# Attention, mixture of experts and gated MLP on one core: the sums of the weights' blocks as GpSimd additions and subtractions instead of adding DMAs and negated copies

## The chip, the cores and the metric

One core of a Trainium2 chip runs the whole program. The metric is device time in microseconds (us), the median of several executions. The engines are named as the profile names them: PE (TensorE; PEld is its weight load), DVE (VectorE), ACT (ScalarE), POOL (GpSimd) and SP (SyncE, which only starts DMAs here).

## The reference, cut to what matters

```python
def reference(q, k, v, moe_w_gate, moe_w1, moe_w2, moe2_w_gate, moe2_w_val, moe2_w_out):
    attn = block_causal_attention(q, k, v)          # 4 batches, 8 heads, 576 positions, head size 64
    x = attn.transpose(0, 2, 1, 3).reshape(2304, 512)
    # mixture of experts: 8 experts, 512 -> 1024 -> 512
    P = np.exp(x @ moe_w_gate - max)                # 8 rounds of normalising rows, then columns
    out = np.zeros((2304, 512), dtype=np.float32)
    for e in range(8):
        h = np.maximum(x @ w1[e], 0.0)
        ye = h @ w2[e]
        out += P[:, e:e + 1] * ye
    # gated MLP: 512 -> 1536 -> 512, weights in float64
    g = out @ w_gate
    return (g / (1 + np.exp(-g)) * (out @ w_val)) @ w_out
```

## The kernel before

The large products are done by a scheme of Strassen and Winograd: a 2x2 arrangement of blocks is multiplied with seven products of blocks instead of eight. For that, four blocks of the weights (`W11`, `W12`, `W21`, `W22`, each 128 partitions x 512 float32) have to be combined into sums `T1` to `T4`. Every operand is then split into a high and a low float16 part: ACT writes the high part (line 146), DVE the low part (line 147), and PE multiplies high by high, high by low and low by high.

The program has three stages. In the first (0 to about 450 us of the span) attention runs, with products of the first two weight units filled in. In the second (about 450 to 1730 us), called the expert stage here, a loop over 14 weight units (half an expert each) interleaves two streams on PE: `products_in` (line 507, into the PSUM tiles `abc`) and `products_out` (line 615, into the tiles `m_o`). A third stream, `Background`, prepares the next unit's weights and, a share per unit, the weights of the gated MLP: one of its small tasks is issued at a step of the loop. The third stage (1730 us on) is the gated MLP.

The order of instructions on each engine is fixed when the program is written out; each engine takes its own in that order and waits on semaphores. A task list per set of weights does this: the loads (`wr`, four DMAs from SP, line 338); four reductions on DVE to the largest value (`wmx`, line 342); `across_begin` (line 101, DVE writes a diagonal, `w_d`, `gg_d`, `gv_d` or `go_d`) and `across_mid` (line 108, a PE product that spreads the maximum over the partitions), so that PE waits in its queue for DVE there; then the scale, and then `sum_tasks` (line 250), which makes the sums in place, each as an adding DMA that POOL issues, between the splits:

```python
        def add(o, x):
            nc.gpsimd.dma_start(o, x, accum_op=ALU.add)
```

An adding DMA can only add, so two of the four blocks are negated by ACT beforehand (`minus`, line 314). A set has five sums. There are 30 sets of expert weights (tiles `wr`) and 9 of the gated MLP (tiles `f_g`, `f_v`, `f_o`; there the operands go back to DRAM by DMAs that SP issues, line 445, `scr_g<-gg`).

POOL also issues the adding DMAs that add each expert's result to the output sum `acc` (lines 1399 and 1411, `acc<-ev_s` and `acc<-ev`). Temporary tiles come from one pool, `Places`, in order of release: who takes a place waits until its last user is done, and that is often one of these DMAs.

Of the kernel before, what the change touches and what calls it, by code (L numbers as in the profile page):

```python
# [13 lines left out]
AF = mybir.ActivationFunctionType  # L14
ALU = mybir.AluOpType
# [10 lines left out]
W11, W21, W22, T4, T1, T2, T3 = range(7)  # L26
# [4 lines left out]
def attention_moe_glu_kernel(  # L31
# [21 lines left out]
    nc = tc.nc  # L53
# [44 lines left out]
    def across_begin(mx, n, name):  # L98
        d = (small if n == 1 else pairs[0]).tile([P, n, P], F32, tag=f"dg{n}", name=f"{name}_d", bufs=1)
        for i in range(n):  # L100
            nc.vector.tensor_scalar_mul(d[:, i], ident, mx[:, i : i + 1])
        return {"d": d, "n": n, "name": name}
# [15 lines left out]
    def pow2_end(g, n, top, name, root=False):  # L118
        r2 = small.tile([P, n], F32, tag=f"sm{n}", name=f"{name}_m")
        nc.vector.tensor_scalar_max(r2, across_end(g), 1e-30)  # L120
        e = small.tile([P, n], F32, tag=f"se{n}", name=f"{name}_e")
        if root:
            nc.vector.tensor_scalar(
                e.bitcast(I32), r2.bitcast(I32), 1, EXPONENT, op0=ALU.logical_shift_right, op1=ALU.bitwise_and
            )
        else:
            nc.vector.tensor_single_scalar(e.bitcast(I32), r2.bitcast(I32), EXPONENT, op=ALU.bitwise_and)
        inv = small.tile([P, n], F32, tag=f"si{n}", name=f"{name}_i")
        nc.vector.tensor_scalar_mul(inv, e, 2.0 ** (-top + (64 if root else 0)))
        s = small.tile([P, n], F32, tag=f"ss{n}", name=f"{name}_s")  # L130
        nc.vector.reciprocal(s, inv)
        return s, inv
# [117 lines left out]
    def sum_tasks(b, sp, name, flip):  # L250

        los = {}

        def add(o, x):
            nc.gpsimd.dma_start(o, x, accum_op=ALU.add)  # L258

        def up(o, src, minus=False):  # L260
            los[o] = sp(o, src, minus)

        def low(o, *gone):
            los.pop(o)()
            places.give(*gone)

        def t0():
            up(W11, b[0][0])

        def t1():  # L270
            low(W11)
            add(b[0][0], b[0][1])
            up(W21, b[1][0], True)

        def t2():
            low(W21)
            add(b[1][0], b[1][1])
            up(W22, b[1][1])

        def t3():  # L280
            low(W22)
            add(b[0][1], b[1][1])

        def t5():
            up(T1, b[0][0], True)
            add(b[1][0], b[0][0])

        def t6():
            low(T1)
            add(b[1][1], b[0][0])  # L290

        def t8():
            up(T3, b[0][1])

        def t9():
            low(T3, b[0][1])
            up(T4, b[1][0], True)
            places.give(b[0][0])

        def t10():  # L300
            low(T4, b[1][0])
            up(T2, b[1][1], flip)

        gap = (0, None, 0)
        return (
            [(1, t0, 0), (1, t1), (1, t2), (0, t3)]
            + [gap] * 1
            + [(1, t5, 0), (0, t6)]
            + [gap] * 2
            + [(1, t8, 0), (1, t9), (1, t10), (0, lambda: low(T2, b[1][1]))]  # L310
        )

    def minus(x):
        nc.scalar.activation(x, x, AF.Copy, scale=-1.0)

    units, made = {}, set()

    def expert_items(u):


        e, f0 = divmod(u * FU, FF)
        inv = small.tile([P, 2], F32, tag="winv", name=f"winv_{u}")
        iw = small.tile([P, 1], F32, tag="iw", name=f"iw_{u}")
        W1, W2 = {}, {}
        units[u] = (W1, W2, iw)
        items = []
        for i, W in enumerate((W1, W2)):
            g = {"b": [[None, None], [None, None]]}

            def load(g=g, i=i):  # L330
                for r in range(2):
                    for c in range(2):
                        b = g["b"][r][c] = places.take(f"wr_{u}_{i}_{r}{c}", F32, main=False)
                        if i == 0:
                            src = w1[e][r * TB : (r + 1) * TB, f0 + c * TB : f0 + (c + 1) * TB]
                        else:
                            src = w2[e, f0 + r * TB : f0 + (r + 1) * TB, c * TB : (c + 1) * TB]
                        nc.sync.dma_start(b, src.rearrange("(k p) f -> p k f", p=P))
                g["mx"] = small.tile([P, 4], F32, tag="wmx", name=f"wmx_{u}_{i}")

            def mx(k, g=g, sums=i == 0 or u >= 2):
                nc.vector.tensor_reduce(
                    g["mx"][:, k : k + 1], g["b"][k // 2][k % 2], axis=AX.XY, op=ALU.max, apply_absolute_value=True
                )
                if sums and k > 1:
                    minus(g["b"][(k - 1) // 2][(k - 1) % 2])

            def begin(g=g, i=i):
                m1 = small.tile([P, 1], F32, tag="wm1", name=f"wm1_{u}_{i}")
                nc.vector.tensor_reduce(m1, g["mx"], axis=AX.X, op=ALU.max)  # L350
                g["r"] = across_begin(m1, 1, f"w{u}{i}")

            def end(g=g, i=i):
                s, iv = pow2_end(g["r"], 1, -1 if i == 0 else 0, f"w{u}{i}")
                g["s"] = small.tile([P, 2], F32, tag="ws", name=f"ws_{u}_{i}")
                nc.vector.tensor_copy(g["s"][:, 0:1], s)
                nc.vector.tensor_scalar_mul(g["s"][:, 1:2], s, -1.0)
                nc.vector.tensor_copy(inv[:, i : i + 1], iv)
                if i == 1:
                    nc.vector.tensor_mul(iw, inv[:, 0:1], inv[:, 1:2])  # L360

            def sp(o, src, minus=False, g=g, i=i, W=W):
                W[o] = places.take(f"w{i}_{u}_{o}", main=False)
                return split_later(W[o][:, 0], W[o][:, 1], src, g["s"][:, minus : minus + 1])

            tasks = [(0, lambda k=k, mx=mx: mx(k), 1) for k in range(3)]
            tasks += [(0, lambda mx=mx, begin=begin: (mx(3), begin()), 1)]
            tasks += [(0, lambda g=g: across_mid(g["r"]), 1), (0, end, 1)]
            if i == 1 and u < 2:

                def plain_sp(r, c, g=g, sp=sp):
                    sp((r, c), g["b"][r][c])()
                    places.give(g["b"][r][c])

                tasks += [(1, lambda r=r, c=c, f=plain_sp: f(r, c)) for r in range(2) for c in range(2)]
            else:
                tasks += sum_tasks(g["b"], sp, f"w{i}_{u}", i == 1)
            tasks.append((0, lambda i=i: made.add((u, i))))
            items.append((4, load, tasks))
        return items  # L380
# [3 lines left out]
    def glu_items(name, src, rawp):  # L384
# [5 lines left out]
        g = {}  # L390
# [11 lines left out]
        def mx(b, r, c):  # L402
            k = 2 * r + c
            if k == 0:
                g["mx"] = small.tile([P, 4], F32, tag="wmx", name=f"gmx_{name}")
            nc.vector.tensor_reduce(
                g["mx"][:, k : k + 1], b[r][c], axis=AX.XY, op=ALU.max, apply_absolute_value=True
            )
# [41 lines left out]
        for t, r, c in quads:  # L450
            if (r, c) == (0, 0):
                b = [[None, None], [None, None]]
            cur = {}

            def last(cur=cur, b=b, r=r, c=c):
                mx(b, r, c)

            def first(cur=cur, b=b, q=(t, r, c)):
                exponent(cur, b, *q)
                if q[1:] == (1, 0):  # L460
                    minus(b[0][1])
                elif q[1:] == (1, 1):
                    minus(b[1][0])

            tasks = [(1, first, 0)]
            tasks += [(0, lambda cur=cur: (shift(cur), sign(cur))), (0, lambda cur=cur: mantissa(cur)), (0, last, 2)]
            if (r, c) == (1, 1):
                tasks[-1] = (0, lambda last=last, t=t: (last(), begin(t)))
                tasks += [(0, lambda: across_mid(g["r"]), 0), (0, lambda t=t: end(t))]
                tasks += sum_tasks(b, lambda o, src, minus=False, t=t: sp(t, o, src, minus), f"g{name}_{t}", name == "o")  # L470
            items.append((0, lambda cur=cur, q=(t, r, c): load(cur, *q), tasks))
# [1250 lines left out]
```

## Time and profile before

| what | value |
|---|---|
| median of 3 executions | 2221.84 us (2218.31 to 2226.15) |
| the profiled execution's own time | 2215.86 us |
| its span | 2214.0 us |
| PE busy | 1991.7 us (90%) |
| DVE busy | 1556.1 us (70%) |
| ACT busy | 1409.3 us (64%) |
| POOL busy | 783.4 us (35%) |
| mean granted clock of PE | 0.969 of full speed |

The time is that of the slowest (here the only) core; the span is the profiled part of it. An engine's busy time is the sum of its instructions, so 90% for PE says that about 222 us of the span pass without a matmul; it does not say what PE waits for then. The granted clock is PE's speed as a share of 2.4 GHz; it has two levels, 1.0 and 0.5 (2.4 and 1.2 GHz).

### The profile page before, as it was taken

What the parts mean: (1) busy time and instruction counts of PE and PEld (TensorE: products, weight loads), DVE (VectorE), ACT (ScalarE), POOL (GpSimd) and SP (SyncE); (2) the same over time, 40 slices, a digit from 0 to 9 for tenths busy, and PEclk for the clock granted to TensorE, in tenths of its full rate; (3) what the DMA queues carried; (4) which work ended last, traced back from release to release, by engine and by line L of the source; (5) the groups of instructions that cost most, each with busy time, mean ns of one, the idle gap of its engine ahead of it and who ended that gap; (6) DMA issues with size and microseconds to landing.
All of it is one profiled execution on the core that took longest, in us unless ns stands there. A gap on an engine that the chain in (4) does not pass through costs nothing. (4 is left out here: it accounts for less than half of the span.)

```text
span 2214.0 us, 47787 instructions
## 1 busy us (share of the span) xinstructions
PE 1991.7 (90%) x18378; PEld 1692.8 (76%) x18378; DVE 1556.1 (70%) x3466; ACT 1409.3 (64%) x3018; POOL 783.4 (35%) x1068
## 2 busy tenths in 40 slices
PE   6789899898989889898998988889898998999997
PEld 3457667787778778787887877778787887888887
DVE  6886774776667666677676677677666787656766
ACT  5666665476767767677776776777677556544442
POOL 4634443123434444444443453434344123100100
PEclk8899999999999999999999999999999999999999
DMA  6533322537898988999898998979889310110212
GB/s 169 129 95 101 105 82 76 136 70 146 167 183 176 182 158 160 188 174 201 148 167 180 173 193 173 190 144 172 181 165 200 94 44 1 44 58 16 63 39 48
DMA packets 196803, 287.56 MB, mean 130 GB/s; under 512 B 19552, under 2 KB 88800, under 8 KB 196576
## 3 DMA queue, kind: packets, MB, share of 16 engines
q0 software_dynamic: 94640, 158.51, 43.2%
q1 hardware_dynamic: 101936, 126.01, 18.8%
q8 instruction: 144, 2.36, 0.4%
q14 instruction: 83, 0.68, 0.1%
HBM read 90.98 MB, written 24.38 MB: 52 GB/s over the span
## 5 line engine op out<-in xcount | busy, mean ns | idle before, releaser
L507 PEld LDWEIGHTS <-w 128*128 128x128 f16 x6720 | 619.7, 100 | 120.2 <-issue 51.9
L615 PEld LDWEIGHTS <-m_h 128*128 128x128 f16 x5292 | 521.2, 99 | 90.4 <-issue 23.0
L507 PE MATMUL abc_m_b<-xs,w 128*128 128x256 f16 (+1 forms) x3840 | 486.8, 268 | 22.4 <-ACT m_t L532 10.0
L1411 POOL DMA_DIRECT2D acc<-ev x351 | 339.6, 1056 | 322.3 <-ACT ev L1418 203.3
L615 PE MATMUL m_o_b<-w,m_h 128*128 128x256 f16 x3024 | 409.7, 275 | 19.3 <-ACT ev L1418 14.6
L615 PE MATMUL m_o_ac<-w,m_h 128*128 128x256 f16 x2268 | 317.3, 277 | 1.1 <-ACT ev L1418 1.1
L147 DVE SCALAR_TENSOR_TENSOR w<-wr,ws,w 128x512 f16<-128x512 f32 x210 | 158.0, 755 | 129.1 <-ACT w L146 124.5
L507 PE MATMUL abc_m_c<-xs,w 128*128 128x256 f16 (+1 forms) x1920 | 230.2, 263 | 16.6 <-ACT m_r L743 13.5
L258 POOL DMA_DIRECT2D wr<-wr x150 | 141.0, 942 | 226.0 <-DMA wr<-wr 72.9
L1418 ACT ACTIVATE ev<-m_o_b,pe 128x256 f32<-128x256 f32 x351 | 161.7, 476 | 74.0 <-PE m_o_b L615 55.8
L146 ACT ACTIVATE w<-wr,ws 128x512 f16<-128x512 f32 x210 | 151.1, 721 | 47.9 <-DMA wr<-wr 34.9
L1418 ACT ACTIVATE ev<-m_o_ac,pe 128x256 f32<-128x256 f32 (+1 forms) x234 | 135.2, 581 | 47.6 <-DMA acc<-ev 23.9
L156 DVE TENSOR_TENSOR m_h<-m_t,m_h 128x512 f16<-128x512 f32 (+1 forms) x210 | 132.8, 635 | 39.6 <-ACT m_h L653 39.0
L650 DVE SCALAR_TENSOR_TENSOR m_h<-m_t,m_h 128x512 f16<-128x512 f32 (+1 forms) x210 | 131.6, 634 | 13.2 <-ACT m_h L646 12.8
L1399 POOL DMA_DIRECT2D acc<-ev_s x65 | 81.1, 1248 | 164.9 <-ACT ev_s L1395 144.1
L966 POOL TENSOR_SCALAR e<-e,r 128x64 f32<-128x64 f32 (+2 forms) x144 | 80.3, 582 | 159.5 <-DVE r L961 100.2
L646 ACT ACTIVATE m_h<-m_t 128x512 f16<-128x512 f32 (+1 forms) x210 | 121.2, 582 | 24.4 <-DVE m_t L529 7.7
L653 ACT CAST m_h<-m_t 128x512 f16<-128x512 f32 (+1 forms) x210 | 122.2, 582 | 20.0 <-DVE m_t L674 9.2
L507 PEld LDWEIGHTS <-gg_w 128*128 128x128 f16 x1260 | 114.0, 98 | 22.7 <-issue 10.7
L615 PEld LDWEIGHTS <-g_h 128*128 128x128 f16 x1134 | 110.5, 98 | 18.4 <-issue 5.4
L507 PEld LDWEIGHTS <-gv_w 128*128 128x128 f16 x1260 | 113.6, 98 | 12.7 <-issue 1.2
L507 PE MATMUL abc_m_a<-xs,w 128*128 128x256 f16 (+1 forms) x960 | 122.0, 269 | 0.0
(320 smaller groups left out, 3463.1 us busy)
## 6 DMA issues: line engine op xcount, KB each, us to landing
acc<-ev POOLq DMA_DIRECT2D x351, 256.0 KB, 5.4
wr<-wr POOLq DMA_DIRECT2D x150, 256.0 KB, 4.5
wr<-in_w_dram SPq DMA_DIRECT2D x128, 256.0 KB, 5.6
acc<-ev_s POOLq DMA_DIRECT2D x52, 256.0 KB, 5.2
st<-hl SPq DMA_DIRECT2D x48, 144.0 KB, 3.5
raw_g<-in_w_gate_dram SPq DMA_DIRECT2D x12, 512.0 KB, 6.0
raw_v<-in_w_val_dram SPq DMA_DIRECT2D x12, 512.0 KB, 5.7
raw_o<-in_w_out_dram SPq DMA_DIRECT2D x12, 512.0 KB, 5.5
```

Source lines behind the costliest of these rows:

```text
L146: nc.scalar.activation(hi, src, AF.Copy, scale=s)
L147: return lambda: nc.vector.scalar_tensor_tensor(lo, src, s, hi, op0=ALU.mult, op1=ALU.subtract)
L156: nc.vector.tensor_sub(lo, src, hi)
L258: nc.gpsimd.dma_start(o, x, accum_op=ALU.add)
L507: nc.tensor.matmul(ps[:, f], W[o][:, sh, k, f * P : (f + 1) * P], xs[:, o, mh, k, c0 : c0 + n], start=x not in begun, stop=True, skip_grou ...
L615: nc.tensor.matmul(ps, h[o][:, sh, k, ii * P : (ii + 1) * P], W[o][:, mh, k], start=o in (X11, X12) and k == 0 and j == 0, stop=True, skip ...
L646: nc.scalar.activation(hi, src, AF.Relu)
L650: nc.vector.scalar_tensor_tensor(lo, src, 0.0, hi, op0=ALU.max, op1=ALU.subtract)
L653: nc.scalar.copy(hi, src)
L1399: nc.gpsimd.dma_start(acc[:, x - ii : x + 1, cols], e[:, :n], accum_op=ALU.add)
L1411: nc.gpsimd.dma_start(acc[:, x], e, accum_op=ALU.add)
L1418: nc.scalar.activation(e[:, cols], ps, AF.Copy, scale=p)
```

## The change

The five sums of a set are made by `tensor_tensor` on POOL, in place, in the same order and at the same places of the task list. Since this operation can subtract, the negated copies on ACT go, and the sign of one split (`W21`) changes with them.

```diff
-        def add(o, x):
-            nc.gpsimd.dma_start(o, x, accum_op=ALU.add)
+        def total(o, x, y, op):
+            nc.gpsimd.tensor_tensor(o, x, y, op=op)
...
         def t1():
             low(W11)
-            add(b[0][0], b[0][1])
-            up(W21, b[1][0], True)
+            total(b[0][0], b[0][0], b[0][1], ALU.subtract)
+            up(W21, b[1][0])
 
         def t2():
             low(W21)
-            add(b[1][0], b[1][1])
+            total(b[1][0], b[1][1], b[1][0], ALU.subtract)
             up(W22, b[1][1])
 
         def t3():
             low(W22)
-            add(b[0][1], b[1][1])
+            total(b[0][1], b[1][1], b[0][1], ALU.subtract)
 
         def t5():
             up(T1, b[0][0], True)
-            add(b[1][0], b[0][0])
+            total(b[1][0], b[1][0], b[0][0], ALU.add)
 
         def t6():
             low(T1)
-            add(b[1][1], b[0][0])
+            total(b[1][1], b[1][1], b[0][0], ALU.add)
...
-    def minus(x):
-        nc.scalar.activation(x, x, AF.Copy, scale=-1.0)
...
-                if sums and k > 1:
-                    minus(g["b"][(k - 1) // 2][(k - 1) % 2])
...
-                if q[1:] == (1, 0):
-                    minus(b[0][1])
-                elif q[1:] == (1, 1):
-                    minus(b[1][0])
```

On POOL, the five sums of the third set of the gated MLP's first weight stood as DMAs between the additions to `acc` (`f_g_00` is the block in row 0, column 0). Before:

```order
L258 DMA f_g_00_10492<-f_g_01_10969 128x512
L1411 DMA acc<-ev_1_2_0_12189 128x512
L258 DMA f_g_10_11048<-f_g_11_12109 128x512
L1411 DMA acc<-ev_1_3_0_12198 128x512
L258 DMA f_g_01_10969<-f_g_11_12109 128x512
L258 DMA f_g_10_11048<-f_g_00_10492 128x512
L258 DMA f_g_11_12109<-f_g_00_10492 128x512
L1399 DMA acc<-ev_1_s_12335 128x2x256
```

The same place of the changed kernel:

```order
L258 TENSOR_TENSOR f_g_00_10468<-f_g_00_10468,f_g_01_10943 128x512
L1402 DMA acc<-ev_1_2_0_12157 128x512
L258 TENSOR_TENSOR f_g_10_11022<-f_g_11_12078,f_g_10_11022 128x512
L1402 DMA acc<-ev_1_3_0_12166 128x512
L258 TENSOR_TENSOR f_g_01_10943<-f_g_11_12078,f_g_01_10943 128x512
L258 TENSOR_TENSOR f_g_10_11022<-f_g_10_11022,f_g_00_10468 128x512
L258 TENSOR_TENSOR f_g_11_12078<-f_g_11_12078,f_g_00_10468 128x512
L1390 DMA acc<-ev_1_s_12303 128x2x256
```

No instruction has moved; each of the 195 sums stands where its DMA stood, and its operand is now computed by POOL itself. On ACT, the place in the expert stage where the third block of the first set of the gated MLP is taken up (line 425), before:

```order
L1418 ACTIVATE ev_1_12_4_7048<-m_o_1_1_ac,pe_6640 128x256
L425 ACTIVATE f_g_10_7059<-raw_g_10_6979 128x512
L314 ACTIVATE f_g_01_6981<-f_g_01_6981 128x512
L1395 ACTIVATE ev_1_s_7074<-m_o_1_0_b,pe_6640 128x256
L646 ACTIVATE m_2_h_7085<-m_2_t_7039 128x512
```

And now, where later lines have numbers that are smaller by 5 or 9:

```order
L1409 ACTIVATE ev_1_12_4_7038<-m_o_1_1_ac,pe_6630 128x256
L420 ACTIVATE f_g_10_7049<-raw_g_10_6969 128x512
L1386 ACTIVATE ev_1_s_7063<-m_o_1_0_b,pe_6630 128x256
L637 ACTIVATE m_2_h_7074<-m_2_t_7029 128x512
```

One copy of 128x512 has gone; there are 78 of them in the program. The rows of PE, DVE and SP are the same in both kernels.

## Rows read from the trace of the kernel before

**Rows 1.** Windows, the expert stage: busy us and instructions of each engine.

```profile
core 0: us, PE busy (x) PEld busy (x) DVE busy (x) ACT busy (x) POOL busy (x), PEclk, DMA share, GB/s
450.00:1730.00 1280.00, 1151.53 (x10643) 1014.47 (x10642) 893.58 (x1759) 910.87 (x1851) 534.12 (x591) 0.97 0.88 171
```

**Rows 2.** PE's waits in the expert stage: us in total, times, longest.

```profile
PE m_w L108 <- DVE w_d L101: 44.4, 13, 6.3
PE m_o_b L615 <- ACT ev L1418: 14.6, 17, 3.8
PE abc_m_c L507 <- ACT m_r L743: 13.5, 7, 2.9
PE abc_m_b L507 <- ACT m_t L532: 10.0, 11, 2.8
PE m_gg L108 <- DVE gg_d L101: 9.1, 3, 3.5
PE m_go L108 <- DVE go_d L101: 8.8, 3, 3.3
PE abc_m_b L507 <- DVE m_t L529: 7.3, 6, 1.9
PE m_gv L108 <- DVE gv_d L101: 7.0, 3, 3.0
```

**Rows 3.** Timeline, 882 to 915 us: start, us, engine, line, [idle before <-releaser].

```profile
882.30 17.52 SPq L445 DMA_DIRECT2D scr_g<-gg  x7
890.07 0.86 POOL L258 DMA_DIRECT2D f_g<-f_g  x1 [2.98 <-DMA f_g<-f_g]
894.14 0.86 POOL L258 DMA_DIRECT2D f_g<-f_g  x1 [3.22 <-PE m_o_b L615]
900.00 7.22 SPq L338 DMA_DIRECT2D wr<-in_w_dram  x4
915.03 0.80 PE L108 MATMUL m_w<-w_d,ones 128*128 128x128 f32 x2 [5.17 <-DVE w_d L101]
```

**Rows 4.** Windows of PE around that wait: us, PE busy, granted clock, DMA share, GB/s.

```profile
905.00:916.00 11.00, 5.83 (x49) 0.90 1.08 243
916.00:921.00 5.00, 5.00 (x36) 0.53 0.28 48
```

**Rows 5.** The page's DMA queues and issues: the software queue, and one sum's DMA.

```profile
q0 software_dynamic: 94640, 158.51, 43.2%
wr<-wr POOLq DMA_DIRECT2D x150, 256.0 KB, 4.5
```

**Rows 6.** Windows of lines 258 (POOL) and 314 (ACT) in the expert stage.

```profile
450.00:1730.00 1280.00, 160.90 (x175) 0.97 0.88 171
450.00:1730.00 1280.00, 43.27 (x70) 0.97 0.88 171
```

**Rows 7.** Waits of POOL and ACT in the expert stage.

```profile
POOL wr L258 <- DMA wr<-wr: 68.6, 38, 6.1
ACT w L146 <- DMA wr<-wr: 33.9, 28, 4.2
```

**Rows 8.** The chain that ended last in the expert stage, shares of 1280 us by line.

```profile
by line: issue 4.0%; DMA wr<-wr 3.9%; DMA acc<-ev 3.5%; DMA acc<-ev_s 2.2%; DMA f_o<-f_o 1.8%; PE abc_m_b L507 1.5%; PE m_o_b L615 1.3%; POOL acc L1411 1.3%; PE m_o_ac L615 1.0%; DMA wr<-in_w_dram 0.6%; ACT ev L1418 0.6%; DMA raw_o<-in_w_ou
```

**Rows 9.** POOL's groups by line and shape: busy us, mean ns | idle before.

```profile
L1589 POOL TENSOR_TENSOR g_t<-v_t,g_t 128x512 f32<-128x512 f32 x12 | 15.3, 1272 | 1.3 <-DVE v_t L529 1.2
```

**Rows 10.** DVE's groups with two SBUF inputs: the largest and the seventh.

```profile
L147 DVE SCALAR_TENSOR_TENSOR w<-wr,ws,w 128x512 f16<-128x512 f32 x210 | 158.0, 755 | 129.1 <-ACT w L146 124.5 <-PE m_o_b L615 2.6 <-PE m_o_ac L615 1.6
...
L156 DVE TENSOR_TENSOR m_h<-m_r,m_h 128x512 f16<-128x512 f32 x56 | 38.3, 684 | 2.0 <-ACT m_h L653 2.0
```

**Rows 11.** Timeline at 1824 us: an operation on POOL and one on DVE.

```profile
1824.42 1.27 POOL L1589 TENSOR_TENSOR g_t<-v_t,g_t 128x512 f32<-128x512 f32 x1 [1.22 <-DVE v_t L529]
1824.98 1.27 DVE L1591 TENSOR_TENSOR g_t<-v_t,g_t 128x512 f32<-128x512 f32 x1
```

**Rows 12.** Line 1591 on DVE, all: ns shortest/median/longest.

```profile
L1591 DVE TENSOR_TENSOR g_t<-v_t,g_t x30: 424/692/1266, 1820.6 to 2193.4; 128x512 f32<-128x512 f32 x24, 128x256 f32<-128x256 f32 x6
```

More of the change, by code (lines that the diff above doesn't have):

```diff
@@ L339, in load, with mx @@
                 g["mx"] = small.tile([P, 4], F32, tag="wmx", name=f"wmx_{u}_{i}")
-            def mx(k, g=g, sums=i == 0 or u >= 2):
+            def mx(k, g=g):
                 nc.vector.tensor_reduce(
```

## The prediction

> **What bounds the kernel now.** I read the busy shares by window first. In the expert stage PE is busy for 1151.5 of 1280 us at a mean granted clock of 0.97, while DVE (894), ACT (911) and POOL (534) are far from full; the DMA engines, on the other hand, are busy for 0.88 of the time [rows 1]. So PE is the bound with holes in it: 1280 - 1151.5 = 128.5 us without a matmul, and a clock of 0.97 costs another 0.03 x 1280 = 38 us. These 167 us are all that this change can win in the stage; the reader should see that the sums lie almost entirely in it (175 of 195) [rows 6].
>
> Next, what PE waits for. The largest part is `across_mid`, whose product waits for DVE to have found the maximum of newly loaded weights: 44.4 + 9.1 + 8.8 + 7.0 = 69.3 us. The next is ACT being late to empty PSUM: 14.6 + 13.5 + 10.0 = 38.1 us in the three largest rows; DVE being late to do so costs 7.3 us [rows 2]. Then I followed one of the long waits back. The product at 915.03 waited 5.17 us for DVE, and DVE for weights whose loads SP had begun to issue at 900.00 and finished 7.2 us later; ahead of them in SP's queue stood seven stores of `gg`, from 882.30 to 899.8; and the last of these stores hang on the last sums, of which POOL issued the fourth after 2.98 us of waiting for an earlier sum's DMA and the fifth after another 3.22 us [rows 3]. (That row names PE as releaser; the product that it names runs all the time, so I take it for the DMA.) Behind the fifth sum in POOL's queue stands an addition to `acc` (the rows of the change show it), whose end frees a place. Between 905 and 916 us the DMA engines are full (1.08), and after the wait the clock is at its lower level, 1.2 GHz, for most of 5 us (0.53) [rows 4]: a long wait is paid for twice.
>
> Last, the chain of waits. From about 1376 us, where it can be followed, to 1730, flights of sums make 3.9% + 1.8% = 5.7% of 1280 us, 73 us, and flights of additions to `acc` 3.5% + 2.2% = 5.7%, as much [rows 8]. The expert stage is thus a PE-bound pipeline that hiccups on DMA latency, and the sums are about half of the latency in that chain.
>
> **What goes.** 175 DMAs of 256 KB in the stage. A sum takes 4.5 us from issue to landing [rows 5]. The software queue took 43.2% of the engines' span for 158.5 MB, and 195 sums move 51.1 MB, which is 32% of it: 0.139 x 2214 = 308 us of all engines, 277 us of it in the stage. The DMA share there should fall from 0.88 to about 0.66. POOL's waits for sums, 68.6 us for `wr` alone, go, and with them the delay of the additions to `acc` behind them; ACT's wait of 33.9 us for them goes as well [rows 7]. ACT also loses 70 copies, 43.3 us [rows 6]; ACT is not the bound, so this counts only through its lateness.
>
> **What comes.** 195 POOL operations of 128x512 float32. The nearest row has the same shape and two SBUF inputs: 1.27 us [rows 9]. The 175 in the stage take 222 us against 161 us for issuing the DMAs [rows 6], so POOL rises from 534 to about 595 of 1280 us. Hidden by POOL's idle time; behind one addition stands at most 1.27 - 0.92 = 0.35 us more, against some 4.5 us less for whoever waits for the sum. The releasers of each sum stay the same splits; no new wait for another engine arises.
>
> The price that the rows do show is DVE's. At 1824.42 us POOL begins a two-input operation; DVE's own two-input operation, begun at 1824.98, takes 1.27 us and ends 0.56 us after POOL's does [rows 11], where its median is 0.69 us [rows 12]. So DVE stands still until POOL is done if both its inputs are in SBUF.
>
> How much is that? Seven groups with two SBUF inputs, from line 147 (158.0 us) to line 156 (38.3 us), 158.0 + 114.9 + 114.5 + 76.7 + 38.7 + 38.5 + 38.3, take 579.6 us, almost all in the stage [rows 10]. At some 0.7 us each these are about 830 in 1280 us, so 0.8 begin within 1.27 us, and each waits half of it on average: about 0.5 us per sum, 88 us of DVE time. Bounds: none (sums that fall into DVE's gaps) and 222 us (all of each). DVE has 386 us idle in the stage, so it does not become the bound; what counts is how much reaches PE. Its lateness to empty PSUM costs PE only 7.3 us today [rows 2], against 894 us of work. I take 12 us, about a seventh; bounds 0 and 88.
>
> In the row it is DVE that waits; POOL's twelve operations of that shape have a mean of 1272 ns, one price for all [rows 9]. The Trainium skill ("SBUF — State Buffer", section "Who interferes with whom") goes further and speaks against this change: between a VectorE instruction with two SBUF inputs and a GpSimd one that reads SBUF, the one that starts second is blocked fully, whichever it is. By that rule a sum that meets DVE at such an operation (579.6 of 1280 us, 0.45 of the time) would first wait for its end and then hold up the next one for its whole 1.27 us: 0.45 x 1.27 + 0.55 x 0.5 = 0.85 us per sum, 148 us of DVE in place of 88, and at the same seventh 21 us of PE, so 9 us more than the sum below.
>
> **The sum,** against the profiled execution's own 2215.9 us. Of the 69 us at `across_mid` I take 40% back, 28 us: the sums are about half of the DMA latency in the chain, but loads and `acc` additions stay. Of the 38 us of clock a third, 12 us, since the slow stretches follow such waits. Of ACT's lateness (38.1 us in the three rows, about 50 with the smaller ones) 30%, 15 us, for the freed copies and waits. Less 12 us for DVE. Bounds of the three gains together: nothing, if loads and `acc` additions alone set the waits, and 69 + 38 + 50 = 157 us if all such waits went. Sum: -28 - 12 - 15 + 12 = -43 us, 2173 us. The 20 sums before 450 us I cost at nothing: POOL's idle time there hides 0.35 us each; without that cover it is 7 us. The profiled execution was 6 us under the median of the runs, so the forecast on their scale is about **2179 us**.
>
> **The rivals.**
> - *It is worth more.* If the sums' flights are what makes the additions to `acc` late too (they stand behind them in POOL's queue and share the DMA engines at 0.88), most of the waits go: 70% of 157 us less 12 gives -98 us, 2124. For it: the waits of POOL [rows 7]; against: the additions to `acc` keep two thirds of the software queue's bytes [rows 5], and the loads stay.
> - *No difference.* The loads wait for places which `acc` additions free, and these wait for ACT, which waits for PE; then shorter sums only make gaps elsewhere. The gains are 12 us, and DVE's price takes them: 2222. For it: half of the chain's flights are not sums [rows 8].
> - *Slower.* DVE's blocking reaches PE. Place: the two-input operations of lines 147, 650, 156 and 674, behind which the operations that empty PSUM (529, 544) stand in DVE's queue. Price: if half of the upper bound, 111 us, arrives at PE against 55 us of gains, +56, 2278; if the 88 us of my estimate arrive, +33, 2255. It decides from 55 / 175 = 0.31 us of PE per sum. Against: in the last stage line 1591's median of 692 ns says that few of its operations are hit [rows 12].
>
> **How the numbers follow.** A measurement of this kernel tells about 0.3% (7 us) from no change. Forecast (-20 to -70 us) 0.45; worth more 0.15; no difference (-20 to +15) 0.20, of which 0.08 lies beyond 0.3% on the fast side and 0.02 on the slow side; slower 0.20. So faster 0.68, same 0.10, slower 0.22. The range leaves out about half of the "worth more" case below 2128 and half of the slower one above 2242. The forecast's own range is 2150 to 2200.
>
> **What would show it.** Right: the stage's DMA share near 0.66; no POOL wait for sums; `across_mid`'s waits near 40 us; a clock of 0.98; DVE busy up by some 90 us in the stage, with maxima near 1.9 us at line 147; POOL's sums at 1.27 us. Wrong: POOL's sums far above 1.27 us because DVE blocks them in turn; `across_mid`'s waits unchanged, which would make the loads' places the cause; or PE's waits for DVE at lines 529 and 544 grown to tens of us.

## The result and the profile after

The changed kernel takes 2246.11 us (median of 4 executions, 2242.41 to 2251.30) against 2223.99 us of the kernel before (4 executions, 2218.31 to 2228.66): a ratio of 1.0102, 95% interval 1.007 to 1.0135. It is slower by 22 us, where 2179 us was forecast and the range ended at 2242. The profiled execution has a span of 2245.0 us, an own time of 2246.76 us and a mean granted clock of 0.960.

The page's busy times come first; they answer to the small table of before.

```profile
PE 2005.3 (89%) x18378; PEld 1697.6 (76%) x18378; DVE 1742.3 (78%) x3466; ACT 1377.8 (61%) x2940; POOL 882.5 (39%) x1068
```

PE's time without a matmul rose from 2214.0 - 1991.7 = 222 us to 2245.0 - 2005.3 = 240 us, and its busy time by 14 us at the same number of matmuls, which goes with the lower mean clock (0.969 before, 0.960 now). What stands out is DVE: the same operations as before take 1742.3 - 1556.1 = 186 us more, 0.95 us for each of the 195 sums. The window of the expert stage answers to [rows 1] (it ends 10 us later here).

```profile
450.00:1740.00 1290.00, 1151.27 (x10601) 1009.56 (x10599) 1061.45 (x1755) 871.44 (x1758) 615.67 (x582) 0.96 0.65 131
```

The DMA share fell from 0.88 to 0.65, as forecast, and PE's clock did not rise: 0.96 against 0.97. Next the page's row for the software queue, which answers to [rows 5], and that of an addition to `acc`, which stood at 5.4 us before.

```profile
q0 software_dynamic: 66560, 107.37, 29.2%
...
acc<-ev POOLq DMA_DIRECT2D x351, 256.0 KB, 4.3
```

So the DMA side did what it should. PE's waits in the expert stage, which answer to [rows 2], show where the time went instead.

```profile
PE m_o_b L606 <- ACT ev L1409: 38.3, 14, 5.9
PE m_w L108 <- DVE w_d L101: 35.2, 18, 4.3
PE abc_m_b L498 <- DVE m_t L520: 32.6, 21, 5.6
PE m_go L108 <- DVE go_d L101: 7.8, 3, 3.3
PE m_gv L108 <- DVE gv_d L101: 7.4, 3, 2.9
PE m_gg L108 <- DVE gg_d L101: 6.8, 3, 3.7
PE abc_m_c L498 <- ACT m_r L734: 3.9, 5, 0.9
PE abc_m_b L498 <- ACT m_t L523: 3.3, 2, 1.8
```

Lines have moved by 9: 498, 520, 606 and 1409 are the former 507, 529, 615 and 1418. `across_mid` fell from 69.3 to 35.2 + 7.8 + 7.4 + 6.8 = 57.2 us. The wait for ACT's emptying of `m_o` went from 14.6 to 38.3 us, that for DVE's of `abc` from 7.3 to 32.6 us, and both have single waits of over 5 us, which they had not before.

What makes DVE late is seen in its groups (busy us, mean ns | idle before) and in all instructions of two lines (shortest/median/longest ns); the first group answers to [rows 10].

```profile
L147 DVE SCALAR_TENSOR_TENSOR w<-wr,ws,w 128x512 f16<-128x512 f32 x210 | 201.8, 966 | 75.0 <-ACT w L146 73.6
L641 DVE SCALAR_TENSOR_TENSOR m_h<-m_t,m_h 128x512 f16<-128x512 f32 x168 | 150.4, 903 | 1.1 <-ACT m_h L637 0.9
...
L665 DVE SCALAR_TENSOR_TENSOR m_t<-m_t,m_t 128x512 f32<-128x512 f32 x112 | 100.5, 897 | 0.8
L339 DVE TENSOR_REDUCE wmx<-wr 128x1 f32<-128x512 f32 x128 | 84.7, 678 | 11.3 <-DMA wr<-in_w_dram 11.1
...
L520 DVE TENSOR_TENSOR m_t<-m_t,abc_m_b 128x512 f32<-128x512 f32 x64 | 43.6, 681 | 26.2 <-PE abc_m_b L498 22.0 <-ACT ev L1409 3.2
```

```profile
L147 DVE SCALAR_TENSOR_TENSOR w<-wr,ws,w x210: 734/747/5931, 27.6 to 1745.3; 128x512 f16<-128x512 f32 x105
L665 DVE SCALAR_TENSOR_TENSOR m_t<-m_t,m_t x140: 410/683/4448, 479.1 to 1826.5; 128x512 f32<-128x512 f32 x112, 128x256 f32<-128x256 f32 x28
L258 POOL TENSOR_TENSOR wr<-wr,wr x150: 1253/1584/2921, 28.9 to 1736.4; 128x512 f32<-128x512 f32 x150
```

Operations with two SBUF inputs grew (line 147 from a mean of 755 to 966 ns, line 641, formerly 650, from 688 to 903). Those with one SBUF input (line 339) or one from PSUM (line 520) kept theirs, 678 and 681 ns. The median of line 147 is still 747 ns, and its longest takes 5.93 us: the price does not come as a little for each operation. Counted in DVE's timeline, 35 operations take 2 us or more, 133.6 us together, where none did before. They hold about half of what DVE lost; the rest lies in about 110 shorter stops. POOL's sums grew as well, to a median of 1.58 us where [rows 9] gave 1.27. The timeline shows one long stop and what hangs on it, on DVE, POOL, ACT and PE, around 874 us.

```profile
873.94 3.41 DVE L665 SCALAR_TENSOR_TENSOR m_t<-m_t,m_t 128x512 f32<-128x512 f32 x1
874.03 2.77 POOL L258 TENSOR_TENSOR wr<-wr,wr 128x512 f32<-128x512 f32 x2
...
877.43 0.62 ACT L644 CAST m_h<-m_t 128x512 f16<-128x512 f32 x1 [3.75 <-issue]
...
878.16 1.58 POOL L258 TENSOR_TENSOR wr<-wr,wr 128x512 f32<-128x512 f32 x1 [1.37 <-DVE w L147]
878.54 1.23 DVE L1365 TENSOR_SCALAR pe<-pr,iw 128x18 f32<-128x18 f32 x1
...
879.87 0.84 ACT L1409 ACTIVATE ev<-m_o_b,pe 128x256 f32<-128x256 f32 x2 [1.82 <-DVE pe L1365]
880.39 1.44 PE L606 MATMUL m_o_b<-w,m_h 128*128 128x256 f16 x6 [5.01 <-ACT ev L1409]
```

DVE's operation of 0.68 us takes 3.41 and ends 0.55 us after the second of two sums that follow each other on POOL; the same distance as in [rows 11], but over two POOL operations in place of one. By the records DVE had begun 0.09 us before the first of them, while in [rows 11] POOL had begun first. ACT's cast waits for DVE's result; behind it stands the emptying of PSUM, which needs a small DVE operation (line 1365), and that came late and was held itself, beside a third sum: 1.23 us in place of a median of 0.23. So an operation with one tile and one number per partition as its inputs can be held too. PE stands still for 5.01 us. Windows of PE (us, PE busy, granted clock, DMA share, GB/s) show what follows.

```profile
868.00:881.00 13.00, 7.99 (x72) 0.91 0.44 73
881.00:885.00 4.00, 4.00 (x20) 0.50 0.28 50
885.00:890.00 5.00, 5.00 (x46) 0.95 0.40 68
```

After the stop PE runs at the lower level, 1.2 GHz, for 4 us: the stop is paid for twice, as in [rows 4], with DVE now in the place of the DMAs.

### The profile page after: what moved, and what is told of

It is laid out like the page before. It is cut to its first block, busy times and chain, and to the rows that moved or that the text cites. A ratio compares the mean times of both kernels' runs of the same rounds, so it can differ in the third digit from the quotient of the medians.

```text
span 2245.0 us, 47504 instructions
## 1 busy us (share of the span) xinstructions
PE 2005.3 (89%) x18378; PEld 1697.6 (76%) x18378; DVE 1742.3 (78%) x3466; ACT 1377.8 (61%) x2940; POOL 882.5 (39%) x1068
## 4 chain that ended last, share of the span: by engine, by line
PE 35%; DVE 23%; issue 7%; ACT 6%; DMA 5%; POOL 1%; SPq 0%; ACTq 0%; DVEq 0%; POOLq 0%
PE m_o_b L606 6%; PE abc_m_b L498 5%; PE m_o_ac L606 4%; DVE m_t L665 3%; DVE m_h L156 3%; PE m_go_b L606 3%; PE abc_g_b L498 3%; PE abc_v_b L498 3%; DVE m_h L641 3%; PE abc_m_c L498 2%; DVE w L147 2%; PE abc_m_a L498 2%; PE m_go_ac L606 2%; DVE wmx L339 2%; DMA wr<-in_w_dram 1%
## 5 line engine op out<-in xcount | busy, mean ns | idle before, releaser
L1402 POOL DMA_DIRECT2D acc<-ev x351 | 318.1, 955 | 367.5 <-ACT ev L1409 273.7
L606 PE MATMUL m_o_b<-w,m_h 128*128 128x256 f16 x3024 | 416.8, 278 | 38.7 <-ACT ev L1409 38.3
L258 POOL TENSOR_TENSOR wr<-wr,wr 128x512 f32<-128x512 f32 x150 | 233.2, 1593 | 138.7 <-DVE w L147 91.4
L147 DVE SCALAR_TENSOR_TENSOR w<-wr,ws,w 128x512 f16<-128x512 f32 x210 | 201.8, 966 | 75.0 <-ACT w L146 73.6
L641 DVE SCALAR_TENSOR_TENSOR m_h<-m_t,m_h 128x512 f16<-128x512 f32 (+1 forms) x210 | 177.2, 854 | 1.1 <-ACT m_h L637 0.9
L156 DVE TENSOR_TENSOR m_h<-m_t,m_h 128x512 f16<-128x512 f32 (+1 forms) x210 | 140.0, 669 | 8.7 <-ACT m_h L644 8.5
L1390 POOL DMA_DIRECT2D acc<-ev_s x65 | 74.7, 1148 | 183.3 <-ACT ev_s L1386 183.3
L498 PE MATMUL abc_m_a<-xs,w 128*128 128x256 f16 (+1 forms) x960 | 127.2, 276 | 0.0
```

The lines of the kernel that those rows point to most:

```text
L147: return lambda: nc.vector.scalar_tensor_tensor(lo, src, s, hi, op0=ALU.mult, op1=ALU.subtract)
L156: nc.vector.tensor_sub(lo, src, hi)
L258: nc.gpsimd.tensor_tensor(o, x, y, op=op)
L498: nc.tensor.matmul(ps[:, f], W[o][:, sh, k, f * P : (f + 1) * P], xs[:, o, mh, k, c0 : c0 + n], start=x not in begun, stop=True, skip_grou ...
L606: nc.tensor.matmul(ps, h[o][:, sh, k, ii * P : (ii + 1) * P], W[o][:, mh, k], start=o in (X11, X12) and k == 0 and j == 0, stop=True, skip ...
L641: nc.vector.scalar_tensor_tensor(lo, src, 0.0, hi, op0=ALU.max, op1=ALU.subtract)
```

## The experiments

The kernel before was timed again beside each group of runs, at 2221.1 to 2225.1 us. Each ratio is against the one beside it; differences between runs of different groups carry these 4 us.

**What the sums cost and what the DMAs had cost.** The first two kernels put the sums of the changed kernel nowhere, and on DVE.

```diff
 def total(o, x, y, op):
-    nc.gpsimd.tensor_tensor(o, x, y, op=op)
+    pass                                         # e1
+    nc.vector.tensor_tensor(o, x, y, op=op)      # e2
```

> The changed kernel with the sums left out altogether (neither POOL operations, nor adding DMAs, nor negated copies), so the later splits read plain blocks; its time shows what freeing the DMA queue and ACT is worth when nothing is paid for it. Theory 'port' (the gain is real, and POOL's sums take it and more by stopping DVE): 2180 to 2195 us, DVE's line 147 back at about 755 ns, PE's waits for DVE at line 520 below 10 us. Rival 'no gain' (freed DMAs and copies are worth nothing, so a small price was enough): 2215 to 2225 us. Rival 'POOL queue' (POOL's longer occupation delays the additions to acc) gives the same 2180 to 2195 us here.

> The changed kernel with the same 195 sums computed on DVE instead of POOL. Theory 'port': DVE pays 195 x 0.69 = 134 us for them in place of the 186 us by which its busy time rose, and no instruction of it is stretched: between the kernel without sums and the changed kernel, 2205 to 2230 us. Rival 'POOL queue': POOL is free again, so close to the kernel without sums, 2185 to 2200 us. Rival 'no gain': 2235 to 2260 us, since DVE's work grows by nearly as much as it was held up.

Without sums: 2125.45 us, 0.9566 [0.9534, 0.9597]. So without their adding DMAs and copies the program is 96 us faster, and POOL's additions cost 2246.1 - 2125.5 = 121 us, 0.62 us for each of 195. The page of this kernel:

```profile
PE 1972.6 (93%) x18378; PEld 1684.4 (79%) x18378; DVE 1550.9 (73%) x3466; ACT 1376.8 (65%) x2940; POOL 610.5 (29%) x873
```

Between this and the changed kernel DVE's busy time differs by 1742.3 - 1550.9 = 191 us, and the span by 118 us: 86 us of PE's standing still (2126.6 - 1972.6 = 154 against 240) and 33 us of PE's busy time. PE's waits in the stage are

```profile
PE m_w L108 <- DVE w_d L101: 32.4, 16, 4.2
...
PE m_o_b L606 <- ACT ev L1409: 4.0, 4, 1.3
PE abc_m_b L498 <- DVE m_t L520: 3.8, 4, 1.3
```

so the sums on POOL account for the growth of the last two, from 4.0 to 38.3 and from 3.8 to 32.6 us.

With the sums on DVE: 2161.33 us, 0.9728 [0.9699, 0.9758]. There they take 0.69 us each, and nothing else on DVE gets longer:

```profile
L258 DVE TENSOR_TENSOR wr<-wr,wr 128x512 f32<-128x512 f32 x150 | 103.5, 691 | 2.1
...
L147 DVE SCALAR_TENSOR_TENSOR w<-wr,ws,w 128x512 f16<-128x512 f32 x210 | 156.4, 748 | 65.2 <-ACT w L146 63.9 <-PE m_o_ac L606 0.7
```

The engine that POOL was to relieve does the work for 36 us of the program's time, where POOL needs 121. Both times lie below every range expected: the ranges were built on a gain of 26 to 41 us from the freed DMAs and copies, where it is 96.

**POOL's reading or POOL's time.** The third kernel leaves the adding DMAs of before and puts idle additions on POOL beside them; the fourth takes the changed kernel and replaces each sum by work for POOL that only writes. (`lsb` has one buffer here to make room.)

```diff
 def add(o, x):                                   # e3, in the kernel before
+    wide = ones.unsqueeze(1).to_broadcast([P, 2, P])
+    for _ in range(2):
+        nc.gpsimd.tensor_tensor(idle, wide, wide, op=ALU.add)
     nc.gpsimd.dma_start(o, x, accum_op=ALU.add)
...
 def total(o, x, y, op):                          # e4, in the changed kernel
-    nc.gpsimd.tensor_tensor(o, x, y, op=op)
+    for _ in range(4):
+        nc.gpsimd.memset(idle, 1.0)
```

> The kernel before, DMAs and negated copies kept, with two idle POOL operations of 128x256 (two SBUF inputs, a constant; about 1.3 us together) ahead of each adding DMA; the result is not changed by them. Theory 'port': the price by itself, without the gain: DVE's line 147 at 950 ns or more, DVE busy up by about 190 us, 2260 to 2290 us. Rival 'POOL queue': slower too, 2250 to 2280 us, but with DVE's operations at their old durations. Rival 'no gain' (the change's whole effect is the price): 2240 to 2250 us.

> The changed kernel with each sum replaced by four memsets of 128x256 on POOL into an idle tile (about 1.2 us together); the sums are left out, as in the first run, but POOL is as busy as with them, writing SBUF without reading it. Theory 'port' (POOL's reads are what stops DVE's second input): DVE's operations at their old durations and 2180 to 2200 us, as without sums. Rival 'POOL queue': 2235 to 2250 us, as in the changed kernel. Between: the write side of the port stops DVE too, then DVE's operations are stretched.

The idle additions make the kernel before 4.7% slower: 2323.99 us, 1.0467 [1.0428, 1.0506], 103 us, with line 147 (149 there) at a mean of 994 ns and DVE busy for 158 us more. That is above the range expected, 2260 to 2290 us; these additions also hold back the DMAs that stand behind them in POOL's queue. The memsets cost next to nothing: 2129.44 us, 0.9586 [0.9558, 0.9613], 4 us over no sums at all. The page of the kernel with memsets, and its groups of POOL and DVE:

```profile
PE 1967.9 (92%) x18378; PEld 1682.2 (79%) x18378; DVE 1553.1 (73%) x3467; ACT 1376.1 (65%) x2940; POOL 855.1 (40%) x1653
```

```profile
L261 POOL MEMSET idle<- 128x256 f16 x780 | 280.7, 360 | 38.3
...
L149 DVE SCALAR_TENSOR_TENSOR w<-wr,ws,w 128x512 f16<-128x512 f32 x210 | 156.0, 748 | 87.7 <-ACT w L148 86.3 <-PE m_o_ac L609 0.7
```

POOL is as busy as in the changed kernel (855 against 882 us), and DVE's line 149 has its old 748 ns. So it is not POOL's occupancy that costs the time, nor the queue behind it. What stretches DVE's operations is that POOL reads SBUF. The kernel with memsets also has no sums for the splits to wait for; how much of the 121 us comes from sums that are late, beside DVE's lost time, these two runs don't part. The Trainium skill ("SBUF — State Buffer", section "Who interferes with whom") has a VectorE instruction with two SBUF inputs contend with a GpSimd instruction that reads SBUF and not with one that only writes it; these two runs agree, with 994 against 748 ns.

**Which part of the old way was dear.** The next two start from the kernel before: one leaves out the copies, the other the adding DMAs.

```diff
 def minus(x):                                    # e5
-    nc.scalar.activation(x, x, AF.Copy, scale=-1.0)
+    pass
...
 def add(o, x):                                   # e6
-    nc.gpsimd.dma_start(o, x, accum_op=ALU.add)
+    pass
```

> The kernel before with the 78 negated copies on ACT left out (the sums, still by DMA, get wrong signs; no other instruction changes). The kernel without sums at all was 96 us faster than before; this splits that gain. Theory 'DMA' (the adding DMAs' flights and traffic hold the stage up, ACT's 49 us of copies do not): 2200 to 2215 us. Rival 'copies' (ACT is what makes PE wait): 2160 to 2185 us.

> The kernel before with the 195 adding DMAs left out and the 78 negated copies kept: the other part of the split, the sums again left out. Theory 'DMA': 2130 to 2150 us, nearly all of the 96 us. Rival 'copies': 2170 to 2205 us.

Without the copies: 2222.84 us, 0.9996 [0.9981, 1.0012]. Without the DMAs: 2130.48 us, 0.9571 [0.9547, 0.9596]. The DMAs hold the whole gain, about 94 us; ACT's 78 copies are worth nothing that can be measured, where 2200 to 2215 us was expected.

Then the DMAs were parted: three of the five sums on DVE and the last two (of `t5` and `t6`) still as adding DMAs; and the kernel before without those last two.

```diff
 def total(o, x, y, op):                          # e7, in the changed kernel
-    nc.gpsimd.tensor_tensor(o, x, y, op=op)
+    nc.vector.tensor_tensor(o, x, y, op=op)
...
-    total(b[1][0], b[1][0], b[0][0], ALU.add)
+    nc.gpsimd.dma_start(b[1][0], b[0][0], accum_op=ALU.add)
...
-    total(b[1][1], b[1][1], b[0][0], ALU.add)
+    nc.gpsimd.dma_start(b[1][1], b[0][0], accum_op=ALU.add)
```

```diff
     up(T1, b[0][0], True)                        # e11, in the kernel before
-    add(b[1][0], b[0][0])
...
     low(T1)
-    add(b[1][1], b[0][0])
```

> The sums on DVE, except the last two of each set (the two plain additions), which are adding DMAs as before; no negated copies. DVE does 117 sums (80 us) instead of 195 (134 us), and 78 DMAs come back. If DVE's 134 us are the larger rest: faster than all sums on DVE, 2140 to 2158 us. If a DMA's flight costs more than 0.69 us of DVE: 2165 to 2200 us; by the price per DMA that the run without sums shows (96 us / 195 = 0.49 us) against that of a DVE sum (36 / 195 = 0.18 us): 2161 + 78 x 0.31 = 2185 us.

> The kernel before with the last two sums of each set left out (78 of 195 DMAs), the first three and the negated copies kept; those two sums are left out of the result. If each DMA costs the same (91 us over 195): 2224 - 36 = 2188 us. If the first three are the dear ones, which the run with three sums on DVE and two by DMA suggests: 2200 to 2220 us. If the last two are dear (they wait for the flights of the first): 2135 to 2165 us.

The first gave 2160.53 us, 0.9705 [0.9683, 0.9727], the same as all five on DVE; its expectation by a price per DMA was missed. The second gave 2163.61 us, 0.9726 [0.97, 0.9753]: two of five DMAs are worth 60 of the 94 us. Yet with the first three on DVE the last two cost no more than on DVE. The DMAs' prices do not add up; with all five by DMA, leaving out the last two saves 60 us, and moving the first three to DVE saves 64 us, DVE's price for them included. So neither part is the dear one by itself; five by DMA are dear. By what (the DMA engines' load, or the row of waits in POOL's queue) was not told apart.

**`across_mid`.** The eighth kernel has the sums on DVE and two empty steps ahead of each `across_mid` in the task lists.

```diff
 tasks += [(0, lambda mx=mx, begin=begin: (mx(3), begin()), 1)]
+tasks += [(0, None)] * 2
 tasks += [(0, lambda g=g: across_mid(g["r"]), 1), (0, end, 1)]
...
+tasks += [(0, None)] * 2
 tasks += [(0, lambda: across_mid(g["r"]), 0), (0, lambda t=t: end(t))]
```

> All sums on DVE, and two empty steps more between DVE's diagonal (across_begin) and PE's product with it (across_mid), so that PE reaches the product later; nothing else is moved by hand. If PE's waits there (about 60 us of the stage also without any sums) come from the two steps standing side by side in the task list: the rows of m_w, m_gg, m_gv and m_go below 25 us together and 2125 to 2150 us. If they come from late loads, as the prediction had it: the rows stay and 2155 to 2168 us.

It is the fastest of all: 2123.51 us, 0.9547 [0.9527, 0.9566], 38 us under the same kernel without the empty steps. Of PE's waits at `across_mid` in the stage (38.1 + 7.3 + 6.4 + 6.0 = 57.8 us there) only one is left:

```profile
PE m_w L108 <- DVE w_d L101: 1.8, 1, 1.8
```

The run does not part the two theories as its expectation has it, since PE that comes later also waits less for a late load. The trace of the kernel without the empty steps does: DVE had waited for a load of `wr` in the 7 us or so before 5.5 of the 57.8 us, ACT for a load of the gated MLP's weights before 13.4 us, and nobody for a load before the other 38.7 us. Those came from PE's product being written out right behind DVE's work for it, and the two steps took all three kinds away. PE's waits for DVE at line 520 and ACT at line 1409 rose by 15 us, from 25.5 to 40.4, which is part of why only 38 us are left of the 56. The waits at `across_mid` stand at 53 us with no sums at all (32.4 + 7.3 + 7.0 + 6.4).

**How DVE's lost time reaches PE.** The sums take 121 us for 191 us of DVE's time. Two theories: any time taken from DVE costs so much, or long stops cost more than the same time in small pieces. The ninth kernel takes DVE's time at the sums' places without POOL, by a sum and an idle addition on DVE; the tenth cuts each of POOL's sums in four; the twelfth puts a memset behind each sum; the thirteenth lets each sum start only when DVE has come to its place in the program, so that sums don't run in rows.

```diff
 def total(o, x, y, op):
-    nc.gpsimd.tensor_tensor(o, x, y, op=op)
+    nc.vector.tensor_tensor(o, x, y, op=op)                            # e9
+    nc.vector.tensor_tensor(idle, ones, ones, op=op)
...
+    for k in range(2):                                                 # e10
+        for c in (slice(0, P), slice(P, 2 * P)):
+            nc.gpsimd.tensor_tensor(o[:, k, c], x[:, k, c], y[:, k, c], op=op)
...
+    nc.gpsimd.tensor_tensor(o, x, y, op=op)                            # e12
+    nc.gpsimd.memset(idle, 1.0)
...
+    nc.vector.tensor_copy(flag[:, 1:2], flag[:, 0:1])                  # e13
+    nc.gpsimd.memset(flag[:, 0:1], 1.0)
+    nc.gpsimd.tensor_tensor(o, x, y, op=op)
```

> All sums on DVE, each followed by an idle DVE operation of 128x128 (0.28 us), which makes DVE's extra work 195 x 0.97 = 189 us, as much as the 186 us by which DVE's busy time rose with the sums on POOL. If DVE's lost time as such is the price of the change: close to the changed kernel, 2215 to 2250 us. If it matters where and in what lumps DVE loses it (at any operation that happens to meet a sum, or only at the sum's place): well below, 2165 to 2195 us (2161 plus 55 us at the 0.27 of PE per us of DVE that the sums on DVE cost).

> The changed kernel with each POOL sum cut into four of 128x128 (about 0.46 us each by itself, 1.8 us together instead of 1.27). If DVE is stopped for whole POOL instructions and long stops are what hurts: shorter stops, 2195 to 2235 us. If only POOL's total time of reading counts: 2250 to 2300 us, with DVE's busy time above 1742 us.

> The changed kernel with a small memset (128x128, 0.2 us, written to an idle tile, nothing read) behind each of POOL's sums. In the changed kernel a DVE operation is seen to stand still over two or three sums in a row (line 665: up to 4.45 us instead of 0.68), where POOL has several sums queued one behind the other. If these long stops over rows of sums are what reaches PE: DVE gets in at the memset, the longest stop falls to about 2.3 us and the time to 2200 to 2232 us. If DVE's lost time counts whatever its lumps are, or POOL's own time does: 2240 to 2260 us. If the memset leaves POOL's read lock unbroken: longest stops of over 4 us as before, and 2244 to 2255 us, which would tell nothing on the lumps.

> The changed kernel, where each POOL sum waits until DVE has come to the sum's place in its own order (DVE copies one number there, POOL overwrites it before the sum), so that sums cannot pile up and run in a row while DVE stands at an earlier operation. If the long stops over rows of sums are what reaches PE: DVE's stops above 2 us (35 in the changed kernel) become rare and the time falls to 2195 to 2232 us (the sums on DVE with as much lost DVE time gave 2193). If the lost DVE time counts whatever its lumps are: 2240 us or more, also with the long stops gone. If the long stops stay, the run tells nothing on this.

The ninth took 2192.86 us, 0.9862 [0.9826, 0.9899]. Its page:

```profile
PE 1989.2 (91%) x18378; PEld 1690.4 (77%) x18378; DVE 1705.5 (78%) x3856; ACT 1379.6 (63%) x2940; POOL 611.2 (28%) x873
```

The added operations last 195 x (0.69 + 0.29) = 191 us, but adjoining ones overlap in the records, and DVE's busy time grew by 1705.5 - 1550.9 = 155 us. That cost 67 us, 0.44 per us of busy time, against 121 / 191 = 0.63 for POOL's sums. It isn't a straight line: from 115 to 155 us of DVE (the second kernel to the ninth) 40 us cost 31.5. Carried on at that slope, 191 us would cost about 97, an estimate; 24 us less than POOL's sums do.

The tenth was slower still, 2280.64 us, 1.0250 [1.022, 1.028]. DVE's stops got shorter at line 667 (the former 665) but not at line 147, and POOL's pieces now took up to 4.39 us (line 260; shortest/median/longest ns):

```profile
L667 DVE SCALAR_TENSOR_TENSOR m_t<-m_t,m_t x140: 411/685/2684, 475.8 to 1860.1; 128x512 f32<-128x512 f32 x112, 128x256 f32<-128x256 f32 x28
L147 DVE SCALAR_TENSOR_TENSOR w<-wr,ws,w x210: 740/752/5872, 29.9 to 1779.4; 128x512 f16<-128x512 f32 x105
L260 POOL TENSOR_TENSOR wr<-wr,wr x600: 442/727/4390, 30.8 to 1774.8; 128x128 f32<-128x128 f32 x150
```

Operations of 2 us or more on DVE fell only from 35 to 27 (133.6 to 106.3 us together), so the shorter stops that were to be tried hardly came about. The 150 sums of `wr` kept POOL busy for 369.9 us, 2.47 us each, where it was 233.2 us, 1.55 each, in the changed kernel. DVE was busy for less (1701.2 us) and yet the program was 34 us slower than the changed kernel; I take it for the lateness of the sums, which was not tried by itself.

The twelfth, 2255.38 us, 1.0152 [1.0125, 1.018], tells nothing on the theories, as its expectation set out: a memset behind a sum did not let DVE in, and line 667's longest is still 4.48 us.

The thirteenth is 1.9 points below the changed kernel: 2207.09 us, 0.9914 [0.9892, 0.9935], though it adds 28 us of copies to DVE. Its groups, lines 669 and 645 (the former 665 and 641), and PE's waits in the stage:

```profile
L260 DVE COPY flag<-flag 128x1 f32<-128x1 f32 x195 | 27.9, 143 | 3.8 <-POOL flag L261 3.8
...
L262 POOL TENSOR_TENSOR wr<-wr,wr 128x512 f32<-128x512 f32 x150 | 215.9, 1440 | 3.2 <-PE m_o_b L610 0.2
...
L669 DVE SCALAR_TENSOR_TENSOR m_t<-m_t,m_t x140: 408/682/693, 473.1 to 1778.8; 128x512 f32<-128x512 f32 x112, 128x256 f32<-128x256 f32 x28
L645 DVE SCALAR_TENSOR_TENSOR m_h<-m_t,m_h x210: 408/684/3248, 463.7 to 1775.8; 128x512 f16<-128x512 f32 x84, 128x256 f16<-128x256 f32 x21
```

```profile
PE m_o_b L610 <- ACT ev L1413: 19.6, 15, 3.0
PE abc_m_b L502 <- DVE m_t L524: 11.3, 6, 2.8
```

Counted in DVE's timeline, operations of 2 us or more fell from 35 (133.6 us together) to 8 (22.8 us). The operations of line 669 on `m_t` alone are never held; the longest stop is now 3.25 us, at line 645. Shorter stops took the place of the long ones: the mean of line 149 (the former 147) is 957 ns, against 966 in the changed kernel. The two waits of PE fell from 38.3 + 32.6 = 70.9 to 30.9 us, and DVE's busy time from 1742.3 to 1708.2. The price over no sums is 82 us for 157 us of DVE's time, 0.52 per us, near the ninth kernel's 0.44. So both theories hold a part: of the 39 us that the thirteenth won back, 34 us less of DVE's time make 27 at the slope above, and some 12 are left for the stops being shorter. The split rests on that slope and is argued, not shown. What is shown is that the same sums on POOL cost 39 us less when each waits for DVE's place. The third kernel speaks against the length of the stops as the main thing: it has a single operation of 2 us or more and yet lost 103 us for 158 us of DVE's time, 0.65 per us, though its delayed DMAs have a share in that.

## Why the prediction was wrong

**What bounds the kernel**, a PE pipeline that hiccups on the sums' DMAs, was right, and the gain was undersized: 96 us in place of 55. By its three terms, against the kernel without sums: `across_mid` gave 69.3 - 53.1 = 16 us (28 were taken); the clock of the stage rose to 0.99, which is 38 us less 0.01 x 1210, so 26 (12 taken); the waits for ACT in the three rows of [rows 2], 38.1 us, fell to 4.0 + 1.1 + 0.2 = 5.3, so 33 (15 taken). The rest of the 96 us was not followed. The rival "worth more" took 110 us for these gains, 98 after its 12 us for DVE.

**The reason given for `across_mid` holds for a third of it.** "Late loads" were read from one wait of 5.17 us [rows 3, 4] and put in for all 69.3 us. DVE's waits for the loads in the stage, before and without sums:

```profile
DVE wmx L342 <- DMA wr<-in_w_dram: 22.0, 15, 3.6
...
DVE wmx L339 <- DMA wr<-in_w_dram: 10.5, 10, 1.8
```

Before, they stand ahead of five of PE's waits, 23.2 us together, the one of 5.17 us among them; without sums the same five make 6.4 us. That is the whole gain of 16 us. Loads of the gated MLP's weights stand ahead of 12.9 us (14.4 without sums), and the 33 us with no late load ahead of them stayed (32). So the 40% were taken of a sum of which two thirds did not move, and it fell out as 23%. Two empty steps took away most of what had stayed (56 of 57.8 us).

**The price of POOL's sums is the step that failed.** In the prediction's words: "Its lateness to empty PSUM costs PE only 7.3 us today [rows 2], against 894 us of work. I take 12 us, about a seventh; bounds 0 and 88." Measured: 121 us, above the bound, with the lateness of POOL's own sums in it. Two errors multiply. DVE lost not 0.5 us per sum but 0.95 (0.98 against no sums). One mean delay per sum leaves out that DVE, once held, can stay held over further sums; [rows 11] could not show it, since a single POOL operation stood alone there. And for each us of DVE's time the program lost not a seventh but 0.63. No row gave the seventh: the 7.3 us beside it are the waits for a DVE without such stops, and for DVE's own emptying of PSUM alone. ACT, which waits for DVE's results, is late with it, and its emptying of `m_o` made the larger wait, 38.3 us. The kernels with more work on DVE (0.31 per us in the second, 0.44 in the ninth) show that a seventh would have been too little even without long stops.

**POOL's sums at 1.27 us** was wrong; those of `wr` took 1.59 us in the mean, with up to 2.92. POOL waits for DVE in turn: the 18 of the 195 sums that met no two-input operation of lines 147, 156, 641 or 665 have a mean of 1.35 us, the others 1.60. That was among the signs written down as "wrong". The rule of the Trainium skill that the prediction weighed ("SBUF — State Buffer", "Who interferes with whom"), by which the second to start waits, whichever it is, is borne out in that each engine holds up the other. That it is the second is not borne out by the records: the operation at 873.94 us had begun before the sums that it waited for, and of DVE's 35 long stops 22 began with no sum running (POOL's spans are rough). The estimate from it of 0.85 us of DVE per sum was nearer to the measured 0.95 than the 0.5 that was taken.

**The 20 sums before 450 us** were costed at nothing. The product `m_lm` towards the end of that stretch starts at 391.0 us, where it started at 385.3 before and starts at 386.5 without sums: they cost 4.5 us against no sums.

**The rival "slower" is what happened**, at the places it named: DVE's blocking at lines 147, 641 and 665 (the former 650 and 674) reaches PE through the emptying of PSUM. That its 2255 us comes near the measured 2246 is luck: the gain is 96 us in place of 55 and the price 121 in place of 88, and the two errors nearly cancel. It put the point that decides at 0.31 us of PE per sum, from a gain of 55 us; measured are 0.62, and a gain of 96, which moves that point to 96 / 195 = 0.49. It had 0.20 as its chance. What the prediction lists as signs came out as: DMA share 0.65 (right), no waits of POOL for sums (right, but its waits for DVE's line 147 at the sums of `wr` rose from 35.9 to 87.9 us), `across_mid` 57 (40 forecast), clock 0.96 (0.98 forecast), DVE in the stage 1061 against 894 (+168, +90 forecast), line 147's longest 5.93 us (1.9 forecast), PE's wait at line 520 at 33 us (the sign of "wrong").

**What is open.** Why three DMAs less take the price of the other two away; and how much of the remaining 82 us of the thirteenth kernel is DVE's time and how much the lateness of POOL's own sums.

## What to carry to other kernels

Work on POOL that reads SBUF has to be priced against every DVE operation with two SBUF inputs, and in rows: ask how many POOL operations can follow each other while DVE stands (here up to three sums in one stop, and 39 us of the price went when each sum waited for DVE's place). Before work is moved to a less busy engine, run the kernel without that work and with it on the busy one; here DVE did the sums for 36 us and POOL for 121. Where an in-order engine waits for a result that is written out just ahead of it, two empty steps can be worth more than the change itself (38 us here).

## What was not expected of the hardware

- A DVE operation of 0.68 us with two SBUF inputs was held for 3.41 us while two POOL additions ran one after the other; the longest took 5.93 us. A memset on POOL between them did not let it in (longest 4.48 us), while with a wait for DVE's place ahead of each sum the longest stop was 3.25 us.
- Cutting POOL's operations in four shortened DVE's longest stop at that line from 4.45 to 2.68 us, but not at line 147 (5.87 us), and POOL's own pieces of 0.44 us at the shortest then took up to 4.39 us.
- POOL's memsets, 281 us of them, cost DVE nothing that shows (748 ns at line 147's operation with them and 749 without sums) and the program 4 us.
